# The last store of a decode block: 32 partitions, every fourth one, in place of all 128

## The chip, the cores and the metric

The kernel runs on one core of one Trainium2 chip. The metric is the device time of one execution in microseconds (us). Before the change it is 242.45 us, the median of three runs (242.36 to 242.57). A profile, taken by the hardware profiler from one execution, gives when each instruction of each engine ran, what it waited for, and when the transfers moved. The engines are PE (TensorE), DVE (VectorE), ACT (ScalarE), POOL (GpSimd) and SP (SyncE); SPq in a row is SP's instruction queue, from which this kernel starts nearly all its transfers.

## The reference, cut to what matters

One decode step of a transformer block for four sequences (B = 4) of one token with D = 512. A condition `c` gives six vectors per sequence that scale, shift and gate two branches: attention over a window of 2048 cached keys, and a gated feed-forward layer.

```python
mod = (_silu(c) @ w_mod).reshape(c.shape[0], 6, 1, -1)
sa, ca, ga, sb, cb, gb = (mod[:, 0], mod[:, 1], mod[:, 2], mod[:, 3], mod[:, 4], mod[:, 5])
h = _layernorm(x, axis=-1) * (1 + ca) + sa
x = x + ga * _A_ref(h, A_k_cache, A_v_cache, A_wq, A_wo)   # 32 heads, 8 groups, head size 128
h = _layernorm(x, axis=-1) * (1 + cb) + sb
x = x + gb * _B_ref(h, B_w1, B_w3, B_w2)                   # silu(h @ w1) * (h @ w3) @ w2
return x                                                   # (4, 1, 512), float32
```

The output has 4 x 512 float32 numbers, 8 KB. The inputs that must be read, keys and values above all, are some 101 MB.

## The kernel before

Everything is float32. `Program` (lines 42 to 143) collects operations in the order in which the text calls them; each engine executes its own in that order, and semaphores are worked out from which operations touch the same memory. So the order on a queue is the order of the calls.

The inputs are read in large transfers into `ring`, a buffer of 192 KB in each partition that is used as three slots; all but one of them go through SP's queue. A transfer into a slot waits until the slot's former contents have been used. In the order of time the stages are: the modulation and the queries (from `w_mod_a` and `wq`); eight groups of attention (`group`, lines 332 to 370; `kv_in`, then `last_k_wo` and `last_v`); the projection of the heads (`project_out`); the second norm; the two input products of the feed-forward layer (`ffn_in`, with `w1` and `w3`); the output product with `w2`, whose rows are loaded in four transfers.

The results are computed in a layout of 128 partitions: 32 j + 8 b + 4 s holds piece j (of four) and half s (of two) of sequence b, 64 numbers in each. So one partition in four holds a result; the three behind it hold what the products leave there. The last three operations (lines 469 to 471) are a product by the gate on DVE, a sum with the residual on DVE, and the store, `dma_start` from SP's queue, which waits for the sum. `res` is a part of the tile that the profile names `p_sb`; `out` is the output tensor in device memory. Behind the store, SP issues two operations on semaphores: one that clears those it has waited on (line 141), and a wait for the store's sixteen completion counts with a clear behind it (lines 142 and 143). These end the program.

The host takes every fourth row of `out` and puts the pieces in the order of the reference (lines 513 and 514); this lies outside the device time.

Of the kernel before, what the change touches and what calls it, by code (L numbers as in the profile page):

```python
# [3 lines left out]
F32 = mybir.dt.float32  # L4
# [4 lines left out]
B, D, HQ, G, SK, DH, W, FF = 4, 512, 32, 8, 8192, 128, 2048, 1792  # L9
P = 128  # L10
# [135 lines left out]
def block_kernel(nc, w_mod_a, wq, kv_in, wo_mod, last_k_wo, last_v, wo, w1, w3, w2, out):  # L146
# [5 lines left out]
    do = Program(nc)  # L152

    def sb(name, *shape):
        return nc.alloc_sbuf_tensor(name, (P, *shape), F32).ap()
# [81 lines left out]
    ss, ln, r0, ve, a, r = (sb(n, 1) for n in ("ss", "ln", "r0", "ve", "a", "r"))  # L237
# [209 lines left out]
    y_ps, y, res = s_ps[2][:, :H], p_sb[2][:, :H], p_sb[3][:, :H]  # L447
# [20 lines left out]
        add_rows(hidT[:, n], w2_t[:, n], n == W2_CUTS[1], n == NF - 1)  # L468
    do("vector", "tensor_mul", y, y_ps, halves[:, 1])
    do("vector", "tensor_add", res, y, halves[:, 0])  # L470
    do("sync", "dma_start", out, res)
    do.emit()


# [40 lines left out]
```

## Time and profile before

| | |
|---|---|
| time, median of three runs | 242.45 us (242.36 to 242.57) |
| span of the profiled execution, first to last instruction | 241.1 us |
| bytes read, bytes written | 101.20 MB, 0.03 MB |
| busy: PE, DVE, ACT | 146.8, 55.2, 24.0 us |
| last DVE instruction starts | 239.30 us |
| store issued on SP's queue | 239.56 us |

The profile page gives of its execution the span alone; what a run's time has beyond a span (some 1.35 us here, 242.45 - 241.1) lies ahead of the first or behind the last recorded instruction. On the page, a row of digits divides the span into 40 equal slices, each digit a busy share in tenths. The chain of waits is followed back from the last instruction to what released it, again and again. In the views of a stretch of time the DMA share is the mean busy share of the core's 16 DMA engines. A transfer is recorded in packets, each on one DMA engine; a row of DMA issues gives the time from the start of the issuing instruction to the landing, that is to the last completion count.

### The profile page before, as it was taken

The numbers are of one execution on the slowest core, as the hardware profiler recorded it, in microseconds if no ns is written. First come the engines' busy times: TensorE is split into PE (matmuls) and PEld (weight loads), VectorE is DVE, ScalarE is ACT, GpSimd is POOL, SyncE is SP. The second block draws the span as 40 slices with busy tenths as digits, with TensorE's granted clock in tenths as the row PEclk, the third lists the DMA queues.
The fourth block names the chain that finished last, engine by engine and source line by source line (L and its number), as shares of the span: only waits on it lengthen the run. The fifth ranks groups of instructions, "written<-read, shape, count | busy, mean of one in ns | idle before, by whom it ended". The sixth has DMA issues, their size and how long they took to land.

```text
span 241.1 us, 2468 instructions
## 1 busy us (share of the span) xinstructions
PE 146.8 (61%) x1103; PEld 52.8 (22%) x1103; DVE 55.2 (23%) x140; ACT 24.0 (10%) x36; POOL 2.6 (1%) x11
## 2 busy tenths in 40 slices
PE   0000169756782972945767586567296919964876
PEld 0000132213222312201311222221131202422333
DVE  4000220240303124123132124130312014103120
ACT  2000000103003003001200300300300000320100
POOL 3000000000000000000000000000000000000000
PEclk9999997995977799779797589797977997996899
DMA  8999989898989898989999999999999999999993
GB/s 316 414 436 425 500 370 500 351 511 359 511 359 503 370 502 370 489 383 478 391 479 391 478 394 468 402 468 405 457 413 424 435 405 435 407 432 426 416 415 133
DMA packets 2889, 101.38 MB, mean 421 GB/s; under 512 B 448, under 2 KB 448, under 8 KB 704
## 3 DMA queue, kind: packets, MB, share of 16 engines
q1 hardware_dynamic: 2736, 92.85, 89.5%
q10 hardware_dynamic: 144, 8.39, 8.1%
q8 instruction: 8, 0.13, 0.2%
q14 instruction: 1, 0.01, 0.0%
HBM read 101.20 MB, written 0.03 MB: 420 GB/s over the span
## 4 chain that ended last, share of the span: by engine, by line
DMA 73%; PE 20%; DVE 3%; ACT 2%; issue 0%; SPq 0%
DMA ring<-kv_in 30%; DMA ring<-wo_mod 17%; DMA ring<-w 15%; DMA ring<-w_mod_a 11%; PE s_ps L57 8%; PE bank L57 7%; PE o_ps L57 4%; PE a_ps L57 2%; ACT p_sb L57 2%; DVE nm L57 2%; DVE p_sb L57 0%; DVE e L57 0%; DVE sq L57 0%; DVE xc L57 0%; DVE tot L57 0%
## 5 line engine op out<-in xcount | busy, mean ns | idle before, releaser
L57 PE MATMUL s_ps<-ring,qT 128*32 128x512 f32 x256 | 37.0, 731 | 20.2 <-DMA ring<-kv_in 14.7
L57 PE MATMUL bank<-ident,p_sb 128*128 128x128 f32 (+1 forms) x136 | 27.4, 350 | 30.8 <-ACT p_sb L57 30.7
L57 PE MATMUL o_ps<-ring,pT 128*16 128x512 f32 x256 | 37.8, 696 | 0.0
L57 PEld LDWEIGHTS bank<-ident,p_sb 128*128 128x128 f32 (+1 forms) x136 | 19.6, 177 | 51.9 <-ACT p_sb L57 31.7
L57 ACT ACTIVATE p_sb<-s_ps,nm 128x2048 f32<-128x2048 f32 (+1 forms) x11 | 16.5, 1501 | 143.2 <-DVE oT L57 105.2
L57 DVE TENSOR_REDUCE nm<-s_ps 128x1 f32<-128x2048 f32 x7 | 16.0, 2292 | 34.5 <-PE s_ps L57 34.5
L57 DVE COPY pT<-bank 128x64 f32<-128x64 f32 x32 | 7.2, 224 | 56.1 <-PE bank L57 56.1
L57 PEld LDWEIGHTS s_ps<-ring,qT 128*32 128x32 f32 x256 | 9.0, 131 | 47.5 <-issue 20.7
L57 PE MATMUL bank<-ident,xs 128*128 128x128 f32 x1 | 0.5, 473 | 27.8 <-POOL xs L57 27.8
L57 PE MATMUL s_ps<-ring,h2T 128*32 128x512 f32 (+1 forms) x64 | 9.1, 664 | 2.3 <-DMA ring<-w 2.3
L57 PE MATMUL a_ps<-ring,oT 128*4 128x512 f32 x64 | 9.1, 709 | 2.0 <-DMA ring<-wo_mod 2.0
L57 PE MATMUL s_ps<-ring,hT 128*32 128x512 f32 x64 | 8.8, 711 | 0.4 <-DVE hT L57 0.4
L57 PEld LDWEIGHTS o_ps<-ring,pT 128*16 128x16 f32 x256 | 5.4, 98 | 11.6 <-issue 9.2
L57 DVE SCALAR_TENSOR_TENSOR o_own<-o_ps,rl,own 128x512 f32<-128x512 f32 x7 | 5.3, 751 | 11.1 <-PE o_ps L57 11.1
L57 DVE TENSOR_REDUCE o_sum<-o_own 128x128 f32<-128x512 f32 x7 | 7.2, 1029 | 0.2
L57 PE MATMUL bank<-ring,sc 128*32 128x256 f32 (+1 forms) x64 | 7.2, 610 | 0.0
L57 PEld LDWEIGHTS bank<-ident,xs 128*128 128x128 f32 x1 | 0.2, 180 | 27.8 <-POOL xs L57 27.8
L57 DVE TENSOR_SCALAR e<-e 128x16 f32<-128x16 f32 x1 | 0.2, 174 | 23.8 <-ACT e L57 23.8
L57 DVE TENSOR_REDUCE mx<-s_ps 128x1 f32<-128x512 f32 x4 | 2.8, 691 | 7.6 <-PE s_ps L57 7.6
L57 DVE COPY qT<-bank 128x64 f32<-128x64 f32 x8 | 2.2, 277 | 9.8 <-PE bank L57 9.4
L57 PEld LDWEIGHTS s_ps<-ring,h2T 128*32 128x32 f32 x64 | 2.6, 129 | 7.4 <-issue 4.5
L57 PE MATMUL s_ps<-ring,hidT 128*32 128x64 f32 (+1 forms) x126 | 3.7, 262 | 0.3 <-DVE hidT L57 0.3
(93 smaller groups left out, 55.4 us busy)
## 6 DMA issues: line engine op xcount, KB each, us to landing
ring<-w SPq DMA_DIRECT2D x2, 3584.0 KB, 38.3
ring<-last_k_wo SPq DMA_DIRECT2D x1, 6144.0 KB, 30.5
ring<-last_v SPq DMA_DIRECT2D x1, 4096.0 KB, 39.9
ring<-w_mod_a SPq DMA_DIRECT2D x1, 2064.0 KB, 26.6
ring<-wo SPq DMA_DIRECT2D x1, 2048.0 KB, 43.4
ring<-w SPq DMA_DIRECT2D x1, 1792.0 KB, 40.9
ring<-w SPq DMA_DIRECT2D x1, 1024.0 KB, 42.9
ring<-w SPq DMA_DIRECT2D x1, 512.0 KB, 43.7
```

Of the source, the lines that this page charges most:

```text
L57: op = Op(engine, lambda: getattr(getattr(self.nc, engine), method)(*args, **kw), [])
```

## The change

The store takes partitions 0, 4, 8 and so on, 32 of them, and the output tensor has 32 rows in place of 128. Each row is 64 numbers (256 bytes), as before. The host no longer picks every fourth row. The lists of instructions of PE, DVE, ACT and POOL are the same; on SP one row differs, the store, whose form is 32x64 in place of 128x64. It stands at the same place and has the same wait.

```diff
@@ block_kernel @@
     do("vector", "tensor_mul", y, y_ps, halves[:, 1])
     do("vector", "tensor_add", res, y, halves[:, 0])
-    do("sync", "dma_start", out, res)
+    do("sync", "dma_start", out, res[::4])
     do.emit()
@@ kernel @@
-    out = nc.dram_tensor("out", (P, P // 2), F32, kind="ExternalOutput").ap()
+    out = nc.dram_tensor("out", (P // 4, P // 2), F32, kind="ExternalOutput").ap()
     block_kernel(nc, *args, out)
     r = run_bass_kernel_spmd(nc, [arrays], core_ids=[0])
-    y = r.results[0]["out"].reshape(4, B, 2, 4, P // 2)[:, :, :, 0]
+    y = r.results[0]["out"].reshape(4, B, 2, P // 2)
     return np.ascontiguousarray(y.transpose(1, 0, 2, 3)).reshape(B, 1, D)
```

## The prediction

> **What bounds the kernel now.** I read the page's first parts and the chain of waits on it, then the end of the span in order of time, then the DMA engines in the stretch of the store.
>
> ```profile
> span 241.1 us, 2468 instructions
> DMA  8999989898989898989999999999999999999993
> GB/s 316 414 436 425 500 370 500 351 511 359 511 359 503 370 502 370 489 383 478 391 479 391 478 394 468 402 468 405 457 413 424 435 405 435 407 432 426 416 415 133
> HBM read 101.20 MB, written 0.03 MB: 420 GB/s over the span
> DMA 73%; PE 20%; DVE 3%; ACT 2%; issue 0%; SPq 0%
> ```
>
> The DMA engines are busy at eight or nine tenths in every slice but the last. The chain that ended last spends 73% of the span in transfers, 176 us, all of them loads. The change leaves each load and its place in the queue as it was, so what bounds the kernel for the first 239 us isn't touched. What is touched stands in the last slice, where the digit falls to 3: there are no loads left there, only the last computation and the store. The end of the span in order of time shows these (start, duration, engine, operation):
>
> ```profile
> 238.68 0.29 PE L57 MATMUL s_ps<-ring,hidT 128*32 128x64 f32 x8
> 239.05 0.22 DVE L57 TENSOR_TENSOR p_sb<-s_ps,xs 128x64 f32<-128x64 f32 x1 [3.88 <-PE s_ps L57]
> 239.30 0.22 DVE L57 TENSOR_TENSOR p_sb<-p_sb,xs 128x64 f32<-128x64 f32 x1
> 239.56 0.35 SPq L57 DMA_DIRECT2D out<-p_sb  x1
> ```
>
> From 239.56 us on, nothing runs but the store. Everything up to there is a strict sequence, PE, DVE, DVE, and then SP. The waits of SP's queue (total, times, longest) and the DMA issues of the last two microseconds say how the rest is spent:
>
> ```profile
> SPq L143 <- DMA out<-p_sb: 1.0, 1, 1.0
> out<-p_sb SPq DMA_DIRECT2D x1, 32.0 KB, 1.5
> ```
>
> The store lands 1.5 us after its issue began, at 241.06, and SP waits idle for the last 1.0 us of that. No other work covers any of it: a microsecond off the store is a microsecond off the time, and one added is one added. The whole question is how much of these 1.5 us depends on the number of rows.
>
> **The change part by part.** First what the 1.5 us consist of. The DMA view of 240.30 to 240.70 has 40 slices of 10 ns, and below it the packets and their time as a share of 16 engines:
>
> ```profile
> DMA  0000000001334468679989939782661221010000
> DMA packets 144, 0.03 MB, mean 82 GB/s; under 512 B 144, under 2 KB 144, under 8 KB 144
> q1 hardware_dynamic: 144, 0.03, 38.9%
> ```
>
> The first busy slice is the tenth, at 240.39, and the last is the 36th, at 240.66. So the 1.5 us divide into four pieces: the issuing instruction, 239.56 to 239.91 (0.35); a pause of 0.48 until the first packet at 240.39; the packets, 0.27; and 0.40 from the last packet to the landing at 241.06. The 144 packets are nine for each of 16 engines, which is eight rows and one more, where 128 rows / 16 is eight; I read the ninth as the completion count, of which the program waits for sixteen. Their time is 0.389 x 16 x 0.4 us = 2.49 us, or 17 ns each, and 9 x 17 = 0.156 us on one engine. The packets last 0.27 in all, since the engines do not start together: the digits climb for about 0.1 us and fall for about 0.1 us. The engines' starts are spread over 0.27 - 0.16 = 0.11 us.
>
> Removed: 96 of the 128 rows, six of nine packets on each engine if all 16 still share the work. Six packets x 17 ns = 0.10 us off the last engine's turn. This is the one term that the rows price directly.
>
> The spread of the starts: what makes it isn't shown. Bounds: if the engines are handed their rows one engine after the other, and the time for it is by rows, three quarters go, 0.11 x 3/4 = 0.08 us; if it is by engines, nothing. No row is nearer to one end, so I take the middle, 0.04.
>
> Issue and pause, 0.35 + 0.48: below, nothing changes; above, all of it is by rows, and three quarters of 0.83 = 0.62 us go. The nearest rows are SP's other issues. Grouped by tile they have min/median/max in ns:
>
> ```profile
> L57 SPq DMA_DIRECT2D ring<-kv_in x7: 327/328/426, 1.1 to 123.6; - x7
> L57 SPq DMA_DIRECT2D ring<-w x6: 327/438/453, 181.6 to 194.7; - x6
> L57 SPq DMA_DIRECT2D ring<-w_mod_a x1: 362/362/362, 0.7 to 0.7; - x1
> ```
>
> All of these have 128 rows, of 2 KB up to 64 KB, and take 0.33 to 0.45 us; the store took 0.35 with rows of 256 bytes. An issue doesn't depend on bytes. On rows they are silent, but the issue has a floor that looks like a fixed form of work, so I take 0. The difference of 327 to 453 ns between like issues is also the bound for a loss: a source that steps by four partitions could cost up to 0.1 us more to set up.
>
> The last 0.40 us, from the last packet to the landing: above, three quarters would go, 0.30, if the writes queued up at the memory; below, nothing. The engines ended their packets over 0.1 us and the end lies 0.40 behind, so it looks like a delay behind each engine's own last packet rather than a queue that 128 small writes fill. I take 0.
>
> Nothing is added, and nothing is moved: no instruction changes its place, the wait is still the one for the sum, and SP's queue holds nothing behind the store but the two operations on semaphores.
>
> Sum: 0.10 + 0.04 = 0.14 us, rounded up to 0.15. The span goes from 241.06 to 240.91, and the time, with the same 1.39 us around the span, from 242.45 to **242.30 us**, or 0.06%. The bounds of the terms: gains of up to 0.10 + 0.08 + 0.62 + 0.30 = 1.10, against a loss of 0.10 set against the 0.10 of the packets, which is no gain at all. The runs themselves spread over 242.36 to 242.57; a measurement of this kernel can tell about 0.2%, 0.485 us, from no change, and the sum is a third of that.
>
> The Trainium skill bears on the sum in "DMA: Bandwidth & Descriptors", section "Anatomy of one DMA": it fits a transfer, there started by GpSimd, as 2.0 us fixed plus bytes / 436 GB/s, and puts most of the fixed part down to the receipt of the write. By this 24 KB less would be worth 0.055 us, and the time 242.39. The measurement differs from its fixed part: 1.5 us in all here, of which 0.40 lies behind the packets.
>
> **The rivals.**
>
> *The setup goes by rows.* The pause of 0.48 us ahead of the first packet is the writing out of 128 rows' descriptors, and falls with them. Three quarters of it, 0.36, come on top of 0.10 and 0.08: 0.54 us, 241.91, and with the issue by rows too (0.26 more), 241.65. For it speaks that the engines start one after the other, as if someone were handing out work; against it, that the loads of this kernel, with rows up to 256 times as long, show an issue of the same length, and that the pause needs no descriptors to be explained. It passes 0.2% when 0.31 us or more of the 0.83 go.
>
> *The rows are spread badly.* The source now steps by four partitions, and the work could be cut otherwise: fewer engines, or smaller pieces. The place is the busiest DMA engine, and the price is 17 ns for each packet that it has beyond nine, all of it on the path, since nothing covers the store. All 33 on one engine would be 24 x 17 = 0.41 us more, 242.86, still within 0.2%. It decides the sign beyond 0.2% from 29 packets more, 38 in all. Cut into single numbers, 2048 / 16 + 1 = 129 on each engine, 120 x 17 ns = 2.04 us more: 244.49, slower by 0.8%. For it: no transfer of the profile has a stepped source or fewer than 128 rows. Against it: within a row the 64 numbers stay contiguous, and 128 such rows went out in 128 packets.
>
> The Trainium skill has a rule for the number of engines, on the same page under "Why a DMA increments its semaphore by 16 and not by 1": the largest number up to 16 that divides the slowest dimension of both sides. For 32 rows that is 16, three packets on each engine, and not this rival; no run here shows a transfer of 32 rows.
>
> *The loads change their rate.* The output tensor becomes 24 KB smaller, and if other tensors lie elsewhere in memory for it, the loads could run at another rate. The place is the 176 us of loads on the chain. Neighbouring slices on the page pair to 435 GB/s (500 and 370, 511 and 359) or 436.5 (503 and 370), which agree to half a per cent; half a per cent of 176 us is 0.88 us, 243.33 or 241.57. It decides at 0.28%. Against it: no row shows addresses, and the DMA engines are busy nearly without a gap, with the same pattern in pair after pair. The busy times from the start to the store (stretch, length, busy us and count of PE, weight loads, DVE, ACT, POOL, then granted TensorE clock, DMA share, GB/s):
>
> ```profile
> 0.00:239.56 239.56, 146.79 (x1103) 52.76 (x1103) 55.20 (x140) 24.05 (x36) 2.56 (x11) 0.86 0.98 423
> ```
>
> The DMA share is 0.98 at 423 GB/s over all that precedes the store, which looks like the engines' own pace.
>
> **How the numbers follow.** The forecast, a gain of 0 to 0.3 us at the end, has a chance of 0.72. Setup by rows has 0.16, of which 0.12 pass 0.2%. Bad spread has 0.04, counted as slower. Another rate of the loads has 0.08: 0.05 slower, 0.01 faster, 0.02 within. So faster by over 0.2% is 0.12 + 0.01 = 0.13; slower 0.04 + 0.05 = 0.09; within 0.2% the rest, 0.78. The predicted time is the forecast's, 242.30. The range reaches down to 241.85, just below the setup rival with the pause alone, and up to 242.60, where the runs of an unchanged time end; outside are the other rivals' far ends, about 0.15 in all. The forecast's own range is 242.1 to 242.5.
>
> **What would show it right or wrong.** In the profile after: a store of 8 KB with 48 packets, three for each engine; the stretch of packets 0.12 to 0.17 us long instead of 0.27; issue, pause and the piece behind the last packet as they are, 0.35, 0.48 and 0.40, each within 0.05; landing about 1.35 us after the issue; and the store's issue still near 239.56. A pause of 0.15 us would make it the setup rival; more than 48 packets, or packets longer than 0.27 us, the bad spread; an issue of the store that has moved by over 0.3 us with the same instructions, the rate of the loads. The forecast is wrong if the time leaves 242.1 to 242.5 by any of these.

## The result, and the profile after

The changed kernel takes 242.74 us, the median of 21 runs (242.50 to 243.32), beside 242.37 us for the kernel before in the same rounds (21 runs, 242.18 to 242.67). The ratio is 1.0015, with a 95% interval of 1.0009 to 1.0021: 0.2 to 0.5 us slower. The forecast was 0.15 us faster.

The page of the kernel after, first parts, in the order of the lines shown of before:

```profile
span 242.0 us, 2468 instructions
DMA  7999989898989898989898999999999999999992
HBM read 101.20 MB, written 0.01 MB: 418 GB/s over the span
DMA 57%; PE 32%; DVE 5%; ACT 3%; issue 1%; ACTq 0%; DVEq 0%
```

The loads are the same 101.20 MB and keep the DMA engines as full as before; the bytes written fell as they should. The chain runs through PE more than before (32% against 20%), but a chain in which loads and attention take turns can be followed back along either, and the share says little by itself. The end of the span in order of time:

```profile
239.74 0.23 DVE L57 TENSOR_TENSOR p_sb<-s_ps,xs 128x64 f32<-128x64 f32 x1 [3.83 <-PE s_ps L57]
240.00 0.23 DVE L57 TENSOR_TENSOR p_sb<-p_sb,xs 128x64 f32<-128x64 f32 x1
240.25 0.54 SPq L57 DMA_DIRECT2D out<-p_sb  x1
```

Two things differ. The store's issue takes 0.54 us in place of 0.35. And it starts 0.7 us later, at 240.25 in place of 239.56. The second is this one execution: it took 243.32 us, the slowest of the 21, and a kernel with the same store (e4_big_out, below) had its issue at 239.51. What belongs to the change is what comes behind the issue. The DMA view of 1.6 us from the issue's start, 40 slices of 40 ns, of the kernel before:

```profile
DMA  0000000000000000000004798520000000000000
DMA packets 144, 0.03 MB, mean 21 GB/s; under 512 B 144, under 2 KB 144, under 8 KB 144
out<-p_sb SPq DMA_DIRECT2D x1, 32.0 KB, 1.5
```

and of the kernel after:

```profile
DMA  0000000000000000000000000000004221000000
DMA packets 48, 0.01 MB, mean 5 GB/s; under 512 B 48, under 2 KB 48, under 8 KB 48
out<-p_sb SPq DMA_DIRECT2D x1, 8.0 KB, 1.7
```

The packets are a third: 48, of which 32 carry 256 bytes and 16 carry 4, which fits two rows and one completion count on each of 16 engines. Their stretch is shorter. But the first of them comes in the 31st slice in place of the 22nd, some 0.35 us later, and the landing moves from 1.5 to 1.7 us. The change did what it says, and the preparation of the transfer took more than the packets gave back.

The trace's records of the issuing instruction, the packets and the completion counts divide each store to the nanosecond. These are the four pieces that the prediction read from the rows; "packets" is from the first one's start to the last one's end, the 4-byte ones included:

| ns | issue | pause to the first packet | packets | last packet to the last count | sum |
|---|---|---|---|---|---|
| before | 348 | 494 | 275 | 340 | 1457 |
| after | 542 | 648 | 183 | 343 | 1716 |
| difference | +194 | +154 | -92 | +3 | +259 |

The sum is 0.26 us, inside the interval of the timed difference (0.22 to 0.51 us), so the store alone is enough to account for the result; the interval is too wide to say whether anything else adds to it.

### The profile page after: what moved, and what is told of

It is laid out like the page before. It is cut to its first block, busy times and chain, and to the rows that moved or that the text cites. A ratio compares the mean times of both kernels' runs of the same rounds, so it can differ in the third digit from the quotient of the medians.

```text
span 242.0 us, 2468 instructions
## 1 busy us (share of the span) xinstructions
PE 150.5 (62%) x1103; PEld 54.3 (22%) x1103; DVE 55.2 (23%) x140; ACT 24.1 (10%) x36; POOL 2.7 (1%) x11
## 3 DMA queue, kind: packets, MB, share of 16 engines
HBM read 101.20 MB, written 0.01 MB: 418 GB/s over the span
## 4 chain that ended last, share of the span: by engine, by line
DMA 57%; PE 32%; DVE 5%; ACT 3%; issue 1%; ACTq 0%; DVEq 0%
DMA ring<-kv_in 33%; PE s_ps L57 17%; DMA ring<-last_k_wo 13%; DMA ring<-w_mod_a 11%; PE bank L57 8%; PE o_ps L57 5%; ACT p_sb L57 3%; DVE nm L57 2%; ACT work L57 1%; PE a_ps L57 1%; DVE sq L57 0%; DVE h L57 0%; DVE mx L57 0%; DVE mod_a L57 0%; DVE xc L57 0%
## 5 line engine op out<-in xcount | busy, mean ns | idle before, releaser
L57 PE MATMUL s_ps<-ring,qT 128*32 128x512 f32 x256 | 38.4, 753 | 17.7 <-DMA ring<-kv_in 11.7
L57 PE MATMUL bank<-ident,p_sb 128*128 128x128 f32 (+1 forms) x136 | 28.9, 364 | 30.8 <-ACT p_sb L57 30.7
L57 PE MATMUL o_ps<-ring,pT 128*16 128x512 f32 x256 | 38.3, 705 | 0.0
L57 PEld LDWEIGHTS bank<-ident,p_sb 128*128 128x128 f32 (+1 forms) x136 | 21.0, 187 | 52.4 <-ACT p_sb L57 31.7
L57 PE MATMUL s_ps<-ring,h2T 128*32 128x512 f32 (+1 forms) x64 | 10.1, 718 | 0.4 <-DVE h2T L57 0.4
L57 DVE COPY oT<-bank 128x16 f32<-128x16 f32 x8 | 1.3, 167 | 11.8 <-PE bank L57 11.8
```

Of the source, the lines that this page charges most:

```text
L57: op = Op(engine, lambda: getattr(getattr(self.nc, engine), method)(*args, **kw), [])
```

## The experiments

Each experiment changes the store (and the size of the output tensor and the host's reading with it, where the number of rows changes); what comes ahead of it stays, but for one store added in e3_warm. In the code cuts each line with + is a kernel of its own. e2_step2, e3_warm, e4_big_out and e8_act_queue compute what the reference does; the other stores, but for the kernel before again (g4_before_again), leave out results, and only their time is of interest. The kernels whose names begin with f or g ran once each, for the profile, and their times aren't compared. Since the store stands alone at the end, its four pieces can be read from one profile each, free of the noise of the loads. The ratios, where given, are against the kernel before.

### Is it the step, the number of rows, the first of a form, or the loads?

```diff
-    do("sync", "dma_start", out, res[::4])
+    do("sync", "dma_start", out, res[:32])                                  # e1_dense32
+    do("sync", "dma_start", out, res[::2])                                  # e2_step2, out of 64 rows
+    do("sync", "dma_start", out, p_sb[3][::4, : P // 2])                    # e3_warm: added, behind the loads of w2
+    do("sync", "dma_start", out[: P // 4], res[::4])                        # e4_big_out, out of 128 rows
```

> Stores the first 32 partitions in place of every fourth one, so the output holds other numbers than the reference's; the bytes, the rows and the tensor are those of the change. In the change's trace the store's issue took 0.54 us (before 0.35) and the pause to the first packet 0.65 us (before 0.48). Theory 'step': a source that steps by four partitions is set up more slowly. It expects an issue of 0.35 and a landing about 1.35 us after the issue's start, and a time 0.1 us below before. Theory 'rows': any store of other than 128 rows is set up more slowly. It expects an issue of 0.54 and a landing at 1.7 us, as in the change, and a ratio near 1.0015. Theory 'first of its form': whatever differs from the transfers ahead of it on the queue costs once; it expects the same 0.54 and 1.7.

> Stores every second partition, 64 rows, five packets on each engine. 'Step' expects a slow issue of about 0.54 us, since the source is stepped; if the cost grows with the step, something between 0.35 and 0.54. 'Rows' expects 0.54 if any number other than 128 is slow, and something between if the cost depends on how many are missing. A theory in which setup goes by rows, with the change's extra cost from elsewhere, expects less than the change. Landing about 1.75 us after the issue's start if setup is as in the change, since two more packets on each engine are 0.03 us more.

> The change, with one more store of the same form (32 rows, every fourth partition, old contents of the same tile) some 35 us ahead of the last one on the same queue; the last sum waits for it, long after it has landed. 'First of its form' expects the last store's issue at 0.35 us, its landing at about 1.3, and a time below before by 0.1 us or more. 'Step' and 'rows' expect both stores slow, 0.54 and 1.7 us, and a ratio near 1.0015.

> The change's store into the first 32 rows of an output tensor that keeps its 128 rows. If the smaller tensor moves other tensors and slows the loads, this is back at the time of before but for the store's own part; if the whole loss is the store's setup, it is the same as the change: issue 0.54, landing 1.7 us, ratio near 1.0015.

Dense and stepped stores of the same 32 rows, the same bytes and the same tensor differ. SP's instruction for the dense one (min/median/max in ns), and its DMA view of 1.6 us from the issue's start:

```profile
L57 SPq DMA_DIRECT2D out<-p_sb x1: 361/361/361, 239.6 to 239.6; - x1
DMA  0000000000000000000002422000000000000000
out<-p_sb SPq DMA_DIRECT2D x1, 8.0 KB, 1.4
```

The issue is back at 0.36 us and the packets begin in the 22nd slice, as in before, and end earlier. The ratio is 1.0001 (0.9993 to 1.0010). So neither 32 rows in place of 128 nor the smaller tensor costs anything. Every second partition (e2_step2) is as slow as every fourth: issue 537, pause 640 ns, ratio 1.0012 (1.0004 to 1.0021): twice the rows at half the step leave the cost as it was. In e4_big_out the tensor has its old size and the store is as slow as in the change, issue 536 and sum 1715 ns, ratio 1.0012 (1.0003 to 1.0021); here the issue starts where it did in before:

```profile
239.51 0.54 SPq L57 DMA_DIRECT2D out<-p_sb  x1
```

With that the loads are cleared: the loss is there with the old tensor and gone with the new one (e1_dense32). e3_warm had an equal store some 30 us earlier on the same queue. Its two stores as one row, the earlier one taking 542 and the last one 473 ns:

```profile
L57 SPq DMA_DIRECT2D out<-p_sb x2: 473/508/542, 208.7 to 239.8; - x2
```

At most 0.07 us of the 0.19 that the issue grew by are a matter of the first of its form; the pause was 653 ns, unchanged, and the ratio 1.0008 (0.9999 to 1.0017). 'First of its form' fell as the cause. What was left was the step.

### Which step, and is it the step at all?

```diff
-    do("sync", "dma_start", out, res[::4])
+    do("sync", "dma_start", out[::4], res[:32])        # e5_dram_step, out of 128 rows
+    do("sync", "dma_start", out, res[49:81])           # e6_dense_offset
+    do("sync", "dma_start", out, res[:64])             # e7_dense64, out of 64 rows
+    do("scalar", "dma_start", out, res[::4])           # e8_act_queue
```

> Stores the first 32 partitions into every fourth row of an output tensor of 128 rows: the step is on the side of the device memory alone, and the output holds other numbers than the reference's. So far a dense source of 32 rows lands 1.4 us after its issue, a stepped one 1.7, of 32 or 64 rows. Theory 'any step': a stepped pattern on either side is set up slowly; it expects an issue of 0.54 us and a landing at 1.7, ratio near 1.0013. Theory 'step across partitions': only the partitions' step counts; it expects 0.36 and 1.4, ratio near 1.000.

> Stores partitions 49 to 80, dense, in place of every fourth one, so the output holds other numbers than the reference's: an odd start, and rows on both sides of the middle of the partitions. Theory 'step across partitions' expects the fast setup, issue 0.36, landing at 1.4 us, ratio near 1.000. Theory 'alignment' (the fast setup needs a block of partitions that starts at a round number, which a stepped source isn't either) expects 0.54 and 1.7, ratio near 1.0013.

> Stores the first 64 partitions, dense, five packets on each engine; the output holds other numbers than the reference's. If the gain of a dense store is packets alone, at 14 to 17 ns each, it lies between 32 rows (1.39 us from issue to landing) and 128 rows (1.46): about 1.42, with an issue of 0.35 and a pause of 0.49 us as at both. If a part of the setup goes by rows, issue or pause differ between 32, 64 and 128 rows.

> The change's stepped store, issued from ACT's queue in place of SP's. If the slow setup belongs to the stepped transfer, it is slow here too: an issue 0.2 us longer than the 0.39 that ACT's only load takes, and a landing at 1.7 us or later. If it belongs to SP's queue or to what SP has to do with its semaphores at the end, the store lands at 1.4 to 1.5 us.

A step on the side of the device memory costs nothing (issue 360, sum 1394 ns; ratio 0.9996, 0.9988 to 1.0005), nor does an odd first partition (356, 1378; 0.9990, 0.9982 to 0.9999). On ACT's queue the stepped store is slow too (508, pause 660, sum 1700; 1.0006, 0.9997 to 1.0015), so SP isn't special; its issue is 0.12 us longer than ACT's only load (0.39), where 0.2 was expected. All this is as 'step across partitions' expected. But 64 dense partitions, which should have been quick under it, were not:

```profile
L57 SPq DMA_DIRECT2D out<-p_sb x1: 526/526/526, 239.5 to 239.5; - x1
DMA  0000000000000000000000000000034653000000
out<-p_sb SPq DMA_DIRECT2D x1, 16.0 KB, 1.7
```

Issue, pause (642 ns) and landing are those of a stepped store; the ratio is 1.0007 (0.9998 to 1.0016). The expectation of 1.42 us for it was wrong, and the step alone couldn't be the cause.

### Span, rows, or rows of one engine?

```diff
-    do("sync", "dma_start", out, res[::4])
+    do("sync", "dma_start", out, res[:96])             # f1_dense96, out of 96 rows
+    do("sync", "dma_start", out, res[:32:2])           # f2_step2_in32, out of 16 rows
+    do("sync", "dma_start", out, res[:48])             # f3_dense48, out of 48 rows
+    do("sync", "dma_start", out, res[::8])             # f4_step8, out of 16 rows
```

> Stores the first 96 partitions, dense; the output holds other numbers than the reference's. So far (issue / landing after its start): 128 dense 0.35 / 1.46 us; 32 dense 0.36 / 1.39; 64 dense 0.53 / 1.75; every fourth or second partition 0.54 / 1.72. So the step alone isn't it. Theory 'span': quick up to 32 partitions from the first to the last, and for the full 128; slow between. It expects 0.53 and 1.8 us (four more packets on each engine than 32 rows). Theory 'step, and 64 for a reason of its own' expects 0.36 and 1.45 if 96 hasn't that reason.

> Stores every second of the first 32 partitions, 16 rows, one for each engine; the output holds other numbers than the reference's. Stepped, but within 32 partitions. 'Span' expects the quick setup: 0.36 and 1.37 us. 'Step' expects the slow one: 0.54 and 1.7 us.

> Stores the first 48 partitions, dense; the output holds other numbers than the reference's. 'Span' with its bound at 32 expects 0.53 and 1.73 us; a bound at 64 (64 itself slow, less quick), or a cost of 64 rows alone, expects 0.36 and 1.41 us.

> Stores every eighth partition, 16 rows, one for each engine, over a span of 121; the output holds other numbers than the reference's. 'Span' and 'step' both expect 0.54 and 1.7 us. A theory in which the slow part cuts the rows of one engine apart (nothing to cut where an engine has one row) expects 0.36 and 1.37 us.

96 dense partitions are quick (issue 363, pause 491, sum 1478 ns), and so are 48 (361, 496, 1395). 'Span' had both slow, and falls. The two stepped stores of 16 rows are slow (587, 636, 1748 within 32 partitions; 553, 646, 1724 over 121), so a single row for each engine doesn't help either. What remained was odd: dense was quick but for 64 rows, stepped was slow in every run.

### The mark

The programs as built sort the stores. Each transfer instruction in them can carry a mark, `ant_dge_precooked`, that the builder (which turns the kernel's calls into instructions) sets by the form of the pattern. All loads of this kernel carry it, and so do the stores of before, of 32 (from partition 49 too), 48 and 96 dense partitions, and that with a step in the device memory. The stepped stores lack it, and so does the one of 64 dense partitions. To tell the mark from rows and dimensions:

```diff
 # g1_gap128, from the kernel before
-    do("sync", "dma_start", out, res)
+    do("sync", "dma_start", out.rearrange("p (n c) -> p n c", n=2), p_sb[3][:, :P].rearrange("p (n c) -> p n c", n=2)[:, :, : H // 2])
 # g2_gap32, g3_split32, from the change
-    do("sync", "dma_start", out, res[::4])
+    do("sync", "dma_start", out.rearrange("p (n c) -> p n c", n=2), p_sb[3][:32, :P].rearrange("p (n c) -> p n c", n=2)[:, :, : H // 2])
+    do("sync", "dma_start", out, res[:32], max_dma_last_dim=128)
```

> Stores all 128 partitions, dense, but from two pieces of 32 numbers with a gap between them, so the output holds other numbers than the reference's, the bytes stay 32 KB and the packets double to 17 on each engine. The instruction as built lacks the mark that all of the kernel's loads and the store of before carry. Theory 'mark': setup is slow whenever the mark is absent, whatever the rows: issue 0.54 us, pause 0.65 us (0.35 and 0.48 in before). Theory 'rows and step' (128 dense partitions are always quick): 0.35 and 0.48.

> Stores the first 32 partitions from two pieces of 32 numbers with a gap; the output holds other numbers than the reference's; five packets on each engine; no mark. 'Mark' expects issue 0.54 and landing at 1.7 us. 'Rows and step' expects 0.36 and 1.4.

> Stores the first 32 partitions, each row cut into two pieces of 32 numbers without a gap; the output holds other numbers than the reference's; the same rows, pieces and bytes as g2_gap32, also a three-dimensional pattern, but with the mark. 'Mark' expects issue 0.36 and landing at 1.4 us. If three dimensions are what costs, it is as slow as g2_gap32.

> The kernel before, unchanged, for one more profile of its store. All theories expect issue 0.35 and landing at 1.46 us, within 0.03.

g2_gap32 and g3_split32 move as many rows, pieces and bytes, in 80 packets each. As built, they differ in the mark, in the gap in the source, and in how the side of the device memory is written down. Without the mark:

```profile
L57 SPq DMA_DIRECT2D out<-p_sb x1: 682/682/682, 239.4 to 239.4; - x1
DMA  0000000000000000000000000000000003442000
out<-p_sb SPq DMA_DIRECT2D x1, 8.0 KB, 1.9
```

and with it:

```profile
L57 SPq DMA_DIRECT2D out<-p_sb x1: 351/351/351, 239.9 to 239.9; - x1
DMA  0000000000000000000002433100000000000000
out<-p_sb SPq DMA_DIRECT2D x1, 8.0 KB, 1.4
```

0.33 us less in the issue and 0.15 in the pause. And 128 dense partitions without the mark (g1_gap128) are slow: issue 617, pause 642 ns, landing at 2.0 us with 272 packets in place of 144. The kernel before, profiled again, gave 348, 498, 268 and 339 ns, so the pieces of this store repeated within some 10 ns; the differences of 0.15 us and more above are far outside that. The size of the slow issue wasn't foreseen: 0.54 us was expected of g1_gap128 and g2_gap32, and it was 0.62 and 0.68. What sets it within the slow ones is open.

All stores together, from the trace's records (a kernel's last store; "sum" is from the issue's start to the last count):

| store | mark | issue | pause | packets | sum, ns |
|---|---|---|---|---|---|
| before, 128 dense | yes | 348 | 494 | 275 | 1457 |
| e1_dense32 | yes | 361 | 493 | 190 | 1388 |
| e5_dram_step, 32 dense | yes | 360 | 493 | 191 | 1394 |
| e6_dense_offset, 32 dense | yes | 356 | 501 | 176 | 1378 |
| f3_dense48 | yes | 361 | 496 | 196 | 1395 |
| f1_dense96 | yes | 363 | 491 | 275 | 1478 |
| g3_split32 | yes | 351 | 491 | 199 | 1385 |
| after, 32 by step 4 | no | 542 | 648 | 183 | 1716 |
| e4_big_out, 32 by step 4 | no | 536 | 643 | 190 | 1715 |
| e3_warm, 32 by step 4 | no | 473 | 653 | 189 | 1667 |
| e8_act_queue, 32 by step 4 | no | 508 | 660 | 183 | 1700 |
| e2_step2, 64 by step 2 | no | 537 | 640 | 217 | 1731 |
| f2_step2_in32, 16 by step 2 | no | 587 | 636 | 178 | 1748 |
| f4_step8, 16 by step 8 | no | 553 | 646 | 172 | 1724 |
| e7_dense64 | no | 526 | 642 | 238 | 1747 |
| g2_gap32 | no | 682 | 640 | 207 | 1867 |
| g1_gap128 | no | 617 | 642 | 354 | 1968 |

With the mark the issue takes 348 to 363 ns and the pause 491 to 501, whatever the rows. Without it 473 to 682 and 636 to 660. No value lies between. The times agree: the three timed kernels with the mark (e1, e5, e6) have ratios of 0.9990 to 1.0001, 0.9996 on the mean; the six without it (the change, e2, e3, e4, e7, e8) 1.0006 to 1.0015, 1.0010 on the mean. The 0.0014 between is 0.34 us, about the 0.33 us by which the sum of the change exceeds that of e1_dense32.

What isn't shown is the mark acting by itself: a stepped pattern wasn't given it by force, and no dense store of a quick form was run without it, though the builder can be told to leave it off for a whole program. The mark, or the property of the pattern by which the builder sets it, separates every run; which of the two, these runs leave open. No version came out that beats the kernel before and computes the same, since the results lie on every fourth partition; a dense 32 rows would be worth 69 ns (1457 - 1388), 0.03%.

## Why the prediction was wrong

**What bounds the kernel, and the empty end: right.** Nothing covers the store; what was added to its issue and pause came out in the time. One reading was coarse: the landing of 1.5 us was a rounded figure, the trace's records give 1.457, so the last piece is 0.340 us and not 0.40.

**Packets: right.** 0.10 us was put down for six packets on each engine; the stretch of the packets fell by 0.092. 48 packets, 16 of them completion counts by their 4 bytes, fit three on each of 16 engines, so "the rows are spread badly" fell. The rule for the number of engines in the Trainium skill, "DMA: Bandwidth & Descriptors", section "Why a DMA increments its semaphore by 16 and not by 1", gives 16 for 32 rows, and the 48 packets agree.

**Spread of the starts: wrong in size.** 0.04 us was taken as the middle of 0 and 0.08. With two rows on an engine in place of eight the engines' packets still last 183 ns in all, although three packets of 17 ns are some 50 on one engine. The spread did not shrink with the rows (183 - 51 = 132 ns, beside 275 - 9 x 17 = 122 before), and the gain was 0. So the stretch of packets came out above the 0.12 to 0.17 us that the prediction had named as its sign.

**Issue and pause: this is the step that failed.** The prediction took 0 for them, on the grounds that "an issue doesn't depend on bytes" and that it "has a floor that looks like a fixed form of work". It allowed 0.1 us of loss for a stepped source, from the differences between SP's loads, and 0.62 us of gain. It was a loss of 0.35 us, 0.19 in the issue and 0.15 in the pause, against the 0.09 that the packets gave. The rows used as the nearest ones were all of one kind: dense, 128 rows, with the mark. From such rows neither the sign nor the bound of a cost for another kind can be had. The sentence on the bad spread said as much ("no transfer of the profile has a stepped source"), but used it for the packets alone, where it ought to have widened the bound of the setup on the side of a loss. So the range ended at 242.60, 0.14 us below the result.

**The rival "setup goes by rows": wrong, and by the same runs.** Issue and pause are 0.35 and 0.49 us for 32, 48, 96 and 128 dense rows alike.

**The last piece: right**, 340 ns before and 343 after, whatever the number of writes (337 to 355 over all stores).

**The loads' rate: not the cause.** The prediction's sign for it, an issue of the store moved by over 0.3 us, did appear in the one profile after (0.7 us). But the issue is at 239.51 in e4_big_out, with the same store, and at 239.64 in e1_dense32, with the new tensor, beside 239.56 before. The loss is there with the old tensor's size (e4_big_out) and gone with the new one (e1_dense32).

The size as a whole: the change lies within the 0.2% that the prediction named as what can be told; 21 runs of each told 0.15% apart. That the time stayed within 0.2%, which had a chance of 0.78, speaks only for the smallness of the store; the forecast's direction was wrong.

## What to carry to other kernels

The preparation of a transfer, 0.84 us ahead of the first packet here, has two levels in these stores, 0.84 to 0.86 us and 1.13 to 1.32, and more rows don't mean the slower one: 128 and 96 dense rows are quick, 64 dense and 16 stepped ones slow. A smaller store is no gain where its pattern falls from the quick to the slow one; before a transfer on the path that sets the end is cut, look whether the built instruction keeps the mark, and weigh the 15 ns of each packet saved on an engine (92 / 6) against some 0.3 us. Where a profile holds transfers of one kind only, it gives no bound for another kind: leave the range open on both sides there.

## What had not been expected of the hardware

That 64 dense partitions are set up 0.31 us more slowly than 48 or 96 (1168 ns from the issue's start to the first packet, against 857 and 854), and that the pause behind the issue grows too, by 0.15 us, although the issuing instruction has ended by then. That the last packet and the last completion count are 0.34 to 0.36 us apart in every store here, with 16 writes or 256. The Trainium skill, "DMA: Bandwidth & Descriptors", section "Anatomy of one DMA", puts most of the fixed time of a transfer started by GpSimd down to the receipt of the write. In these stores, started by SP and ACT, all that lies behind the last packet is about a quarter of the time or less (340 of 1457 ns in the kernel before), and the setup ahead of the first packet is more than half (842 ns).
